# The first projection of a two-layer transformer kernel: chunk 0 normalized and transposed tile by tile, its weights loaded and split in another way

## Chip, cores, metric

One core of a Trainium2 chip. The metric is the device time of one execution in microseconds (us). Engines are named as in the profile: PE (TensorE matmuls), PEld (its weight loads), DVE (VectorE), ACT (ScalarE), POOL (GpSimd), SP (SyncE, which here only issues DMAs).

## What is computed

Two layers, each an attention block with one key/value head for 16 query heads, then a gated feed-forward block, all in f32, on x of 2048 rows by 448:

```python
x = A_x
for _ in range(2):
    x = x + A(layernorm(x), wq, wk, wv, wo)      # q: 16 heads of 28; k, v: one head of 28
    x = x + B(layernorm(x), w_gate, w_up, w_down) # (silu(g) * u) @ w_down, 1792 wide
```

The same weights serve both layers. The layer norm has no scale or shift: (x - mean) / sqrt(var + 1e-5).

## The kernel before

The 2048 rows are held in `xres` as 16 tiles of 128 rows, in four chunks of four tiles (512 rows). Every f32 matmul is done in three passes over operands split into a high half (rounded to fp32r) and a low half (the remainder): high x high, high x low, low x high. Names with h or hi hold high halves, names with l or lo low ones: `xh`/`xl` the normalized and transposed x of a chunk, `wh`/`wl` the projection's weights.

The order of the work is written out by hand: each engine runs its instructions in the order in which the code records them, and waits in place for what an instruction needs. DMAs are issued by SP and ACT; eight semaphores go round among them all, so that an issue also waits until the transfer that used its semaphore last has landed, and what stands behind it on that engine waits too.

The head of the program, layer 0's first projection, goes like this.

- Loads (L1104 on): the four tiles of chunk 0 of x, two by SP and two by ACT. Then `load_wqkv`: the projection's weights in two sets of 448 rows. Set z = 1 (tile `wr`, columns 224 to 447 of wq, and wk) is issued by ACT, set z = 0 (tile `wq` in the profile, `wq2` in the code; columns 0 to 223 of wq, and wv) by SP. `rows3` (L129) writes 448 rows as three blocks of 128 partitions and a fourth of 64 rows that is written twice, to partitions 0 to 63 and 64 to 127: three transfers a call.
- PE turns the identity 36 times (L1113) before there is any work.
- Normalization of chunk 0 (`norm_steps`, L211): statistics of the four tiles (DVE, L217 and L218), one rstd for all four columns (POOL: add eps at L222, power -0.5 at L223), the four tiles applied (DVE, L230), columns 384 to 447 of each written a second time (POOL, L232), so that block k = 3 holds its 64 rows twice.
- `parts[0]` splits set z = 1: ACT casts to `wh` (L190, once the wq columns, 128x896, once the wk columns, 128x128), POOL subtracts for `wl` (L192).
- `flip` transposes chunk 0 on PE (L248), four tiles for each k, into four PSUM banks; ACT casts each bank to `xh` (L254, L258), DVE subtracts for `xl` (L255) and for the lower half of k = 3 (L264).
- `project` runs the 16 products of the projection, one after the other: chunk c by column block m, order 3, 2, 0, 1 (m = 3 and 2 need set z = 1, m = 0 and 1 set z = 0). `product_T` (L304) is 11 matmuls of 128x512 into one bank. After a product, ACT copies it twice (L539, L540), SP stores it, and for m = 0 and 1 DVE turns 32 rows of it (`vt`, L547) and POOL copies them to `vsb`. Around the last product of a chunk the next chunk is transposed (`turned`): in layer 0 behind the whole of the fourth product with its copies, later ahead of the product. The statistics of chunks 1 to 3 are planned beside earlier products.
- `parts[1]` splits set z = 0: ACT casts, DVE subtracts. POOL fills constants (L1131 to L1138) meanwhile.

Later, attention runs as 128 cycles a layer of scores, exponentials and products with V, and the feed-forward block as 14 weight groups of 128 a layer. Their weights (`weights`) and the reloaded chunks (`fetch`, `back`) are read by `rows3` too. The kernel also holds a second, unshortened version of everything behind a branch that is taken only if a check on the exponentials fails; it is not run here.

Of the kernel before, what the change touches and what calls it, by code (L numbers as in the profile page):

```python
# [8 lines left out]
F32 = mybir.dt.float32  # L9
F32R = mybir.dt.float32r  # L10
AF = mybir.ActivationFunctionType
ALU = mybir.AluOpType
# [43 lines left out]
def forward(  # L56
# [72 lines left out]
    def rows3(dst, src, eng=nc.sync):  # L129
        eng.dma_start(dst[:, 0:3], src[0:384, :].rearrange("(k p) n -> p k n", p=P))  # L130
        for half in (slice(0, 64), slice(64, 128)):
            eng.dma_start(dst[half, 3], src[384:448, :])

# [34 lines left out]
    def load_wqkv(pool, first):  # L168
# [5 lines left out]
        def load(z):  # L174
            if first and not z:
                r = halves("wq2").bitcast(F32).rearrange("p a (b n) -> p (a b) n", n=256)
            else:
                r = wpool.tile([P, 4, 2, P], F32, name="wr").rearrange("p k b n -> p k (b n)")
            nc.gpsimd.memset(r[:, :, 252:256], 0.0)
            eng = nc.scalar if first and z else nc.sync  # L180
            rows3(r[:, :, 0:224], wq[:, 224 * z : 224 * z + 224], eng)
            rows3(r[:, :, 224:252], wk if z else wv, eng)
            return r

        def part(z, r):
            hi, lo = (w[:, :, 256 * z : 256 * z + 256].rearrange("p k (b n) -> p k b n", b=2) for w in (wh, wl))
            for cols, n0, n1 in ((r[:, :, 0:224], 0, 112), (r[:, :, 224:256], 112, 128)):
                raw = cols.rearrange("p k (b n) -> p k b n", b=2)
                if first:
                    nc.scalar.copy(hi[:, :, :, n0:n1], raw)  # L190
                    eng = nc.gpsimd if z else nc.vector
                    eng.tensor_tensor(lo[:, :, :, n0:n1], raw, hi[:, :, :, n0:n1], ALU.subtract)  # L192
                else:
                    split(hi[:, :, :, n0:n1], lo[:, :, :, n0:n1], raw)

        if first:
            r1, r0 = load(1), load(0)
            return [lambda: part(1, r1), lambda: part(0, r0)], (wh, wl)
        for z in (1, 0):
# [103 lines left out]

    def product_T(po, a_h, a_l, tiles):  # L304

        xh, xl = tiles[:2]
        seq = []
        for k in range(3):
            seq += [(a_h[k], xh[:, k, :]), (a_h[k], xl[:, k, :]), (a_l[k], xh[:, k, :])]
        seq += [(a_h[3], xh[:, 3, :]), (a_l[3], xh[:, 3, :])]  # L310
        for i, (a, b) in enumerate(seq):
            nc.tensor.matmul(po, a, b, start=(i == 0), stop=(i == len(seq) - 1))
# [30 lines left out]
    class Attention:  # L343
# [152 lines left out]
        def project(self):  # L496
# [6 lines left out]
            for o in turned if not late else ():  # L503
                self.turned(o)
            self.q(c, m)
            for o in turned if late else ():
                self.turned(o)
            for f in self.plan.get((self.seen, 1), []) + self.when.pop(self.seen, []):
# [6 lines left out]

        def q(self, c, m):
            cs = slice(512 * c, 512 * c + 512)
# [4 lines left out]
            wh, wl = self.w  # L522
            product_T(po, [wh[:, k, ms] for k in range(4)], [wl[:, k, ms] for k in range(4)], self.X[c])
            if not full and self.seen in (6, 10, 14):
# [587 lines left out]
    for n in range(IDLE):  # L1112
        nc.tensor.transpose(idle[:, 0:P], ident, ident)  # L1113
    parts, at.w = load_wqkv(xb.enter_context(tc.tile_pool(name="wqkv0", bufs=1)), True)
    nc.gpsimd.memset(halfn, -0.5)
    nc.scalar.activation(warm, halfn[:, 0:1], AF.Exp)
    nc.gpsimd.memset(bottom, 0.0)
    nc.gpsimd.memset(bottom[0:1, :], 1.0)
    fs, got = norm_steps(0)
    for f in fs[:5]:  # L1120
        f()
    for f in fs[5:]:
        f()
    parts[0]()
    at.norms[0] = got
# [3 lines left out]
    at.X = {c: xtile(xpool if c == 0 else xbp) for c in range(NC)}  # L1129
    at.turned(0)  # L1130
    nc.gpsimd.memset(vsb, 0.0)  # L1131
    nc.gpsimd.memset(vsb[:, :, DH : DH + 1], 1.0)
    nc.gpsimd.memset(qraw, 0.0)
    if mask is not None:
        nc.gpsimd.memset(mask, 0.0)
        nc.gpsimd.memset(mask[:, 0:16:5, :], 1.0)
        for base, sign in ((0, 1), (DH - 1, -1)):
# [3 lines left out]
            )  # L1141
    parts[1]()
    for c in range(1, NC):
# [40 lines left out]
```

## Time and profile before

| | |
|---|---|
| median of 3 runs | 1955.11 us (1954.94, 1955.11, 1956.85) |
| the profiled execution | 1957.93 us, span 1956.2 us |
| mean granted clock of PE | 0.998 |
| busy | PE 99%, PEld 68%, ACT 64%, DVE 50%, POOL 29% |
| PE waits for, up to 70 us, by what they wait for | 1.5 (identity), 1.1, 2.1, 0.7 (two waits), 0.3 us |

A timeline row gives the start from the beginning of the span, the duration (from the first start to the last end where "xN" rows are merged), engine, line, operation, written <- read tiles, and in brackets how long the engine sat idle before it and what ended that. ACTq and SPq are the DMA issues of those engines. A row of stages gives from:to, its length, then for PE, PEld, DVE, ACT and POOL the busy time with the number of instructions, then the granted clock, the DMA share and GB/s. A row of groups gives shapes and count, then busy us and mean ns of one, then the idle time ahead. A row of waits gives total, times, longest.

### The profile page before, as it was taken

Reading aid. Unit: us, or ns where it says so; the run is one execution under the profiler, and the core shown is the slowest. Engines: PE = TensorE matmul, PEld = TensorE weight load, DVE = VectorE, ACT = ScalarE, POOL = GpSimd, SP = SyncE. Lnnn points to the kernel's source line nnn. Section 1 sums busy time; section 2 is a strip of 40 time slices with the busy share of each in tenths; the row PEclk is TensorE's granted clock in tenths of the full one; section 3 lists DMA queues with packets and bytes.
Section 4 is the critical chain, followed back from the end, with each engine's and each line's share of the span. In section 5 each row is a group of like instructions: output and inputs, shape, how many; then the busy total and the mean of one; then the engine's idle time right before and its main releaser. Section 6 shows DMA issues by size and latency. Waiting matters only on the chain. (4 is left out here: it accounts for less than half of the span.)

```text
span 1956.2 us, 43857 instructions
## 1 busy us (share of the span) xinstructions
PE 1938.9 (99%) x18393; PEld 1335.2 (68%) x18393; DVE 976.9 (50%) x1643; ACT 1252.7 (64%) x1871; POOL 559.6 (29%) x596
## 2 busy tenths in 40 slices
PE   8999999999999999999999999999999999999998
PEld 7544544445469999999975445454454699988887
DVE  6665575665744222222655565657656532232323
ACT  4899898998953333333348998989989433333332
POOL 4213123122215333433332221122231252333420
PEclk9999999999999999999999999999999999999999
DMA  5111011021122011100251110110211221011102
GB/s 164 58 34 31 21 39 41 23 58 34 29 80 73 17 32 32 33 24 20 71 151 40 34 33 18 43 37 26 53 52 32 71 63 31 17 32 32 32 2 77
DMA packets 105475, 87.54 MB, mean 45 GB/s; under 512 B 25304, under 2 KB 85464, under 8 KB 105272
## 3 DMA queue, kind: packets, MB, share of 16 engines
q1 hardware_dynamic: 103576, 83.25, 15.1%
q8 instruction: 145, 2.38, 0.5%
q10 hardware_dynamic: 1696, 1.43, 0.2%
q14 instruction: 58, 0.48, 0.1%
HBM read 59.48 MB, written 23.33 MB: 42 GB/s over the span
## 5 line engine op out<-in xcount | busy, mean ns | idle before, releaser
L656 ACT ACTIVATE pt<-three 128x1536 f32<-128x1536 f32 x512 | 725.1, 1492 | 52.7 <-PE three L634 52.7
L689 PE MATMUL bank<-pt,vsb 128*32 128x512 f32 x3072 | 490.8, 598 | 0.0
L689 PE MATMUL bank<-pair,vsb 128*32 128x512 f32 x1024 | 487.3, 598 | 0.6 <-ACT pair L657 0.6
L634 PE MATMUL bank<-qstack,keys 32*128 32x512 f32 x1536 | 473.2, 424 | 0.0
L634 PE MATMUL three<-qstack,keys 32*128 32x512 f32 x4608 | 428.6, 408 | 0.5 <-ACT stage L540 0.3
L634 PEld LDWEIGHTS bank<-qstack,keys 32*128 32x128 f32 x1536 | 243.3, 183 | 250.3 <-issue 124.1
L655 DVE COPY pair<-bank 128x512 f32<-128x512 f32 x512 | 354.2, 692 | 95.1 <-PE bank L634 58.8
L332 PE MATMUL bank<-xh,wgh 64*128 64x512 f32 x1712 | 375.8, 389 | 0.0
L332 PE MATMUL bank<-xh,wgl 64*128 64x512 f32 x1391 | 324.1, 390 | 0.0
L1017 DVE TENSOR_TENSOR sg<-bank,sg 128x512 f32<-128x512 f32 x112 | 77.4, 691 | 491.0 <-ACT sg L1016 486.1
L332 PE MATMUL bank<-wdh,h 64*128 64x448 f32 x1760 | 311.6, 363 | 0.8 <-DVE h L1021 0.5
L657 ACT ACTIVATE pair<-pair 128x1024 f32<-128x1024 f32 x256 | 283.5, 1108 | 0.0
L332 PE MATMUL bank<-xl,wgh 64*128 64x512 f32 x1284 | 282.3, 389 | 0.0
L634 PEld LDWEIGHTS three<-qstack,keys 32*128 32x128 f32 x4608 | 261.1, 183 | 13.9 <-DVE xres L605 1.5
L689 PEld LDWEIGHTS bank<-pt,vsb 128*32 128x32 f32 x3072 | 101.7, 109 | 246.3 <-issue 153.2
L897 POOL TENSOR_TENSOR xres<-stage,xres 128x448 f32<-128x448 f32 x107 | 126.4, 1202 | 480.0 <-ACT stage L896 479.7
L698 DVE TENSOR_TENSOR o<-bank,o 128x512 f32<-128x512 f32 x224 | 154.9, 692 | 203.3 <-PE bank L689 203.3
L339 ACT COPY seen<-bank 128x1 f32<-128x1 f32 x654 | 74.9, 164 | 259.3 <-PE bank L332 258.5
L332 PEld LDWEIGHTS bank<-xh,wgh 64*128 64x128 f32 x1712 | 200.5, 184 | 12.2 <-issue 1.0
L332 PEld LDWEIGHTS bank<-wdh,h 64*128 64x128 f32 x1760 | 198.1, 184 | 11.6 <-issue 1.7
L1016 ACT ACTIVATE sg<-bank 128x512 f32<-128x512 f32 x112 | 67.3, 601 | 214.7 <-PE bank L332 211.5
L332 PE MATMUL bank<-wdl,h 64*128 64x448 f32 x880 | 184.1, 367 | 0.0
(147 smaller groups left out, 2144.7 us busy)
## 6 DMA issues: line engine op xcount, KB each, us to landing
o<-rd SPq DMA_DIRECT2D x32, 256.0 KB
qraw<-qd SPq DMA_DIRECT2D x128, 56.0 KB
xt<-tb SPq DMA_DIRECT2D x32, 224.0 KB
qd<-stage SPq DMA_DIRECT2D x28, 224.0 KB
wdr<-in_B_w_down_dram SPq DMA_DIRECT2D x28, 224.0 KB
xn<-xt SPq DMA_DIRECT2D x8, 768.0 KB
wr<-in_B_w_gate_dram SPq DMA_DIRECT2D x28, 192.0 KB
wr<-in_B_w_up_dram SPq DMA_DIRECT2D x28, 192.0 KB
```

The source lines that it names most:

```text
L332: nc.tensor.matmul(po, a, b, start=start, stop=stop, skip_group_check=True)
L339: nc.scalar.copy(seen[:, i : i + 1], po[:, 0:1])
L634: nc.tensor.matmul(three[:, j, :] if j < 3 else one, k[js, kp, ks], q[js, part, :], start=(z == 0), stop=(z == 2), tile_position=(32 * j, 0),)
L655: copies.append(nc.vector.tensor_copy(pt1, one))
L656: es.append(nc.scalar.activation(pt, threes[y], AF.Exp, scale=SCALE))
L657: es.append(nc.scalar.activation(pair, pair, AF.Exp, scale=SCALE))
L689: nc.tensor.matmul(to[32 * j : 32 * j + 32, :], vsb[:, n % NT, :], pts[n][j], start=(y == 0), stop=(y == 1), skip_group_check=True,)
L698: f = nc.vector.tensor_tensor(accs[i][:, 0, :], to, accs[i][:, 0, :], ALU.add)
L897: nc.gpsimd.tensor_tensor(r, s, r, ALU.add)
L1016: nc.scalar.activation(in_order(sg, True), natural(pg[0], True), AF.Silu)
L1017: nc.vector.tensor_tensor(in_order(sg, True), natural(pg[1], True), in_order(sg, True), ALU.mult)
```

## The change

- `rows3` writes the fourth block by one transfer that reads its 64 rows twice.
- Set z = 1's wq columns are issued by SP ahead of set z = 0; ACT issues only the wk columns.
- Chunk 0 is normalized tile by tile: each tile has its own add and power on a 128x1 column, and is applied as soon as the next tile's statistics are recorded. The second copy of columns 384 to 447 goes from POOL to ACT.
- The casts of set z = 1 stand on ACT between the second and third of these copies; its low halves are subtracted by POOL (wq columns) and DVE (wk columns). Set z = 0 is split on POOL alone, ahead of the constants.
- Chunk 0 is transposed tile by tile, each tile into all four banks.
- In the first product of layer 0 the four matmuls that read `wl` come last (`low_last`).
- Beside the fourth product the transposes and splits of chunk 1 are recorded behind its matmuls, ahead of its copies.

```diff
     def rows3(dst, src, eng=nc.sync):
         eng.dma_start(dst[:, 0:3], src[0:384, :].rearrange("(k p) n -> p k n", p=P))
-        for half in (slice(0, 64), slice(64, 128)):
-            eng.dma_start(dst[half, 3], src[384:448, :])
+        eng.dma_start(dst[:, 3], src[384:448, :][None].to_broadcast([2, 64, src.shape[1]]))
...
-            eng = nc.scalar if first and z else nc.sync
-            rows3(r[:, :, 0:224], wq[:, 224 * z : 224 * z + 224], eng)
-            rows3(r[:, :, 224:252], wk if z else wv, eng)
+            rows3(r[:, :, 0:224], wq[:, 224 * z : 224 * z + 224])
+            rows3(r[:, :, 224:252], wk if z else wv, nc.scalar if first and z else nc.sync)
             return r
 
-        def part(z, r):
+        def part(z, r, low=None):
             hi, lo = (w[:, :, 256 * z : 256 * z + 256].rearrange("p k (b n) -> p k b n", b=2) for w in (wh, wl))
             for cols, n0, n1 in ((r[:, :, 0:224], 0, 112), (r[:, :, 224:256], 112, 128)):
                 raw = cols.rearrange("p k (b n) -> p k b n", b=2)
-                if first:
-                    nc.scalar.copy(hi[:, :, :, n0:n1], raw)
-                    eng = nc.gpsimd if z else nc.vector
-                    eng.tensor_tensor(lo[:, :, :, n0:n1], raw, hi[:, :, :, n0:n1], ALU.subtract)
+                if first and z:
+                    if low is not True:
+                        nc.scalar.copy(hi[:, :, :, n0:n1], raw)
+                    if low is not False:
+                        eng = nc.vector if n0 else nc.gpsimd
+                        eng.tensor_tensor(lo[:, :, :, n0:n1], raw, hi[:, :, :, n0:n1], ALU.subtract)
                 else:
                     split(hi[:, :, :, n0:n1], lo[:, :, :, n0:n1], raw)
 
         if first:
             r1, r0 = load(1), load(0)
-            return [lambda: part(1, r1), lambda: part(0, r0)], (wh, wl)
+            return [lambda: part(1, r1, False), lambda: part(1, r1, True), lambda: part(0, r0)], (wh, wl)
...
-    def product_T(po, a_h, a_l, tiles):
+    def product_T(po, a_h, a_l, tiles, low_last=False):
...
+        if low_last:
+            seq = seq[0:2] + seq[3:5] + seq[6:8] + [seq[9], seq[2], seq[5], seq[8], seq[10]]
...
-            self.q(c, m)
-            for o in turned if late else ():
-                self.turned(o)
+            self.q(c, m, turned if late else ())
...
-            product_T(po, [wh[:, k, ms] for k in range(4)], [wl[:, k, ms] for k in range(4)], self.X[c])
+            product_T(
+                po, [wh[:, k, ms] for k in range(4)], [wl[:, k, ms] for k in range(4)], self.X[c],
+                low_last=self.layer == self.seen == 0,
+            )
+            for o in turned:
+                self.turned(o)
...
-    fs, got = norm_steps(0)
-    for f in fs[:5]:
-        f()
-    for f in fs[5:]:
-        f()
-    parts[0]()
+    fs, got = norm_steps(0, twice=False)
+    got["r"] = pers.tile([P, 4], F32, name="rstd", bufs=2)
+
+    def tile_rstd(t):
+
+        r = got["r"][:, t : t + 1]
+        nc.gpsimd.tensor_scalar(r, mv[:, t, 1:2], 1.0, EPS, ALU.mult, ALU.add)
+        nc.gpsimd.tensor_tensor(r, r, halfn[:, 0:1], ALU.pow)
+
+    def tile_apply(t):
+
+        fs[5 + t]()
+        nc.scalar.copy(got["x"][:, t, D:512], got["x"][:, t, 384:D])
+
+    for t in range(4):
+        fs[t]()
+        tile_rstd(t)
+        if t:
+            tile_apply(t - 1)
+        if t == 2:
+            wparts[0]()
+    tile_apply(3)
+    wparts[1]()
     at.norms[0] = got
...
-    at.turned(0)
+    pts = [bank(wide[-1])[1] for _ in range(4)]
+    for t in range(4):
+        for k in range(4):
+            nc.tensor.transpose(pts[k][:, P * t : P * t + P], got["x"][:, t, P * k : P * k + P], ident)
+    for k in range(4):
+        flipped(at.X[0], k, pts[k], nc.scalar.copy)
+    del at.norms[0]
+    wparts[2]()
...
-    parts[1]()
```

ACT's queue from its first weight issue to the first cast of chunk 0 (`wr` holds set z = 1, `xn` the normalized tiles, bank_87 the transposes of k = 0), before:

```order
L130 DMA wr<-in_A_wq_dram 128x3x224
L132 DMA wr<-in_A_wq_dram 64x224 x2
L130 DMA wr<-in_A_wk_dram 128x3x28
L132 DMA wr<-in_A_wk_dram 64x28 x2
L1116 ACT_TABLE_LOAD
L1116 ACTIVATE warm<-halfn 128x1
L190 CAST wh<-wr 128x4x2x112
L190 CAST wh<-wr 128x4x2x16
L254 CAST xh<-bank_87 128x512
```

and with the change:

```order
L130 DMA wr<-in_A_wk_dram 128x3x28
L131 DMA wr<-in_A_wk_dram 128x1x28
L1121 ACT_TABLE_LOAD
L1121 ACTIVATE warm<-halfn 128x1
L1136 COPY xn<-xn 128x64 x2
L189 CAST wh<-wr 128x4x2x112
L189 CAST wh<-wr 128x4x2x16
L1136 COPY xn<-xn 128x64 x2
L254 CAST xh<-bank_87 128x512
```

Two issues stand ahead of the table load instead of six, and four copies of 64 columns have come in around the two weight casts.

POOL's queue after the first fills (`rstd` is the normalization's factor, `mv` mean and variance, `wq_173` set z = 0), with the change; before, one add and one power on 128x4, the four copies to `xn`, and the two subtractions from `wr` stood ahead of the fills of `vsb`:

```order
L1130 TENSOR_SCALAR rstd<-mv 128x1
L1131 TENSOR_TENSOR rstd<-rstd,halfn 128x1
L192 TENSOR_TENSOR wl<-wr,wh 128x4x2x112
L134 TENSOR_SCALAR wh<-wq_173 128x4x2x112
L135 TENSOR_TENSOR wl<-wq_173,wh 128x4x2x112
L134 TENSOR_SCALAR wh<-wq_173 128x4x2x16
L135 TENSOR_TENSOR wl<-wq_173,wh 128x4x2x16
L1160 MEMSET vsb 128x512
```

The first two rows stand there four times in turn; the four rows on `wq_173` have come from ACT and DVE, ahead of the fills.

DVE's queue at chunk 1 (bank_85 and bank_86 hold the third and fourth product, banks 87, 88, 78, 79 the transposes of chunk 1), before:

```order
L547 STREAM_TRANSPOSE vt<-bank_85 32x512
L547 STREAM_TRANSPOSE vt<-bank_86 32x512
L255 TENSOR_TENSOR xl<-bank_87,xh 128x512
L255 TENSOR_TENSOR xl<-bank_88,xh 128x512
L255 TENSOR_TENSOR xl<-bank_78,xh 128x512
L264 TENSOR_TENSOR xh<-bank_79,xh 64x512
L409 TENSOR_TENSOR kdiag<-few,mask 112x512
```

and with the change:

```order
L552 STREAM_TRANSPOSE vt<-bank_85 32x512
L255 TENSOR_TENSOR xl<-bank_87,xh 128x512
L255 TENSOR_TENSOR xl<-bank_88,xh 128x512
L255 TENSOR_TENSOR xl<-bank_78,xh 128x512
L264 TENSOR_TENSOR xh<-bank_79,xh 64x512
L552 STREAM_TRANSPOSE vt<-bank_86 32x512
L411 TENSOR_TENSOR kdiag<-few,mask 112x512
```

The turn of the fourth product's rows has moved behind the four subtractions; the number of instructions is the same.

More of the change, by code (lines that the diff above doesn't have):

```diff
@@ L514, in turned, with q @@
                 flip(self.norms.pop(c), self.X[c])
-        def q(self, c, m):
+        def q(self, c, m, turned):
             cs = slice(512 * c, 512 * c + 512)
@@ L1113, in forward @@
         nc.tensor.transpose(idle[:, 0:P], ident, ident)
-    parts, at.w = load_wqkv(xb.enter_context(tc.tile_pool(name="wqkv0", bufs=1)), True)
+    wparts, at.w = load_wqkv(xb.enter_context(tc.tile_pool(name="wqkv0", bufs=1)), True)
     nc.gpsimd.memset(halfn, -0.5)
```

## The prediction

> **What bounds the kernel now.** I read the busy shares first, then the stages, then who TensorE (PE) waited for in the first 70 us, then the timeline.
>
> ```profile
> PE 1938.9 (99%) x18393; PEld 1335.2 (68%) x18393; DVE 976.9 (50%) x1643; ACT 1252.7 (64%) x1871; POOL 559.6 (29%) x596
> ```
> ```profile
> 10.00:20.00 10.00, 7.52 (x37) 5.70 (x37) 6.13 (x13) 6.27 (x12) 5.23 (x12) 1.00 0.83 290
> ...
> 70.00:100.00 30.00, 30.00 (x333) 13.28 (x332) 18.44 (x30) 30.00 (x25) 1.90 (x2) 1.00 0.05 14
> ```
> ```profile
> PE bank L312 <- ACT xh L254: 2.1, 1, 2.1
> ...
> PE bank L248 <- DVE xn L230: 1.1, 1, 1.1
> ```
> PE is busy 99% of the span, so only its idle time, or what makes it start later, can be saved by a change that leaves its matmuls alone. At 70 us attention begins with PE and ACT both full (30.00 of 30 us); what is ahead of it is a chain, and a chain that ends earlier moves everything behind it. The change touches that head. Its timeline (start, duration):
>
> ```profile
> 4.24 0.63 DVE L217 BATCH_NORM_STATS2 stats<-xres 128x6 f32<-128x448 f32 x1 [4.24 <-DMA xres<-in_A_x_dram]
> 4.90 0.18 DVE L218 BATCH_NORM_AGGREGATE mv<-stats 128x2 f32<-128x6 f32 x1
> 5.00 0.59 DVE L217 BATCH_NORM_STATS2 stats<-xres 128x6 f32<-128x448 f32 x1
> ...
> 7.08 0.18 DVE L218 BATCH_NORM_AGGREGATE mv<-stats 128x2 f32<-128x6 f32 x1
> 7.35 0.20 POOL L222 TENSOR_SCALAR rstd<-mv 128x4 f32<-128x4 f32 x1 [5.50 <-DVE mv L218]
> 7.64 1.03 POOL L223 TENSOR_TENSOR rstd<-rstd,halfn 128x4 f32<-128x4 f32 x1
> ...
> 8.71 1.78 DVE L230 TENSOR_SCALAR xn<-xres,mv,rstd 128x448 f32<-128x448 f32 x4 [1.44 <-POOL rstd L223]
> ...
> 9.27 0.14 PEld L248 LDWEIGHTS bank<-ident,xn 128*128 128x128 f32 x1 [1.38 <-DVE xn L230]
> ...
> 9.60 1.28 ACT L1116 ACT_TABLE_LOAD   x1 [9.60 <-DMA wr<-in_A_wk_dram]
> 9.70 0.14 PEld L248 LDWEIGHTS bank<-ident,xn 128*128 128x128 f32 x1 [0.29 <-DVE xn L230]
> ...
> 11.00 0.92 ACT L190 CAST wh<-wr 128x896 fp32r<-128x896 f32 x1
> ...
> 13.41 0.30 ACT L190 CAST wh<-wr 128x128 fp32r<-128x128 f32 x1 [1.49 <-DMA wr<-in_A_wk_dram]
> 13.62 1.56 ACT L254 CAST xh<-bank 128x512 fp32r<-128x512 f32 x3
> 14.23 1.89 DVE L255 TENSOR_TENSOR xl<-bank,xh 128x512 fp32r<-128x512 f32 x3 [3.74 <-ACT xh L254]
> ...
> 14.25 0.50 PE L312 MATMUL bank<-xh,wh 128*128 128x512 f32 x1 [2.07 <-ACT xh L254]
> ```
> The wait that ends last is not the normalization. DVE is done with xn at 10.49, but ACT stands behind its own DMA issues until 9.60 and then at a cast that waits for wk until 13.41; the casts of xh are queued behind it, and PE's first product starts at 14.25.
>
> **Part 1: when the first product starts.** ACT now issues four transfers without a wait and has its table loaded long before it is needed. What is late next is the last tile's normalization. The unknown is the power on 128x1. By the L222 row nothing there is under 0.20; the 128x4 power took 1.03, and these are the ends. Between them:
>
> ```profile
> L232 POOL COPY xn<-xn 128x64 f32<-128x64 f32 x16 | 5.8, 388 | 2.7 <-DVE xn L230 2.7
> ...
> L550 POOL COPY vsb<-vt 32x64 f32<-32x64 f32 x16 | 3.7, 234 | 5.7 <-DVE vt L547 5.1
> ...
> L192 POOL TENSOR_TENSOR wl<-wr,wh 128x896 fp32r<-128x896 f32 x1 | 2.1, 2072 | 1.2 <-ACT wh L190 1.2
> ...
> L192 POOL TENSOR_TENSOR wl<-wr,wh 128x128 fp32r<-128x128 f32 x1 | 0.5, 458 | 0.0
> ```
> The two L192 rows give (2072 - 458) / 768 = 2.1 ns a column and 0.19 us fixed. If the rest of the power's 1.03, 0.84, goes by element, one costs 0.21, and the instruction 0.40. I take 0.40, nearest to the rows of the same operation. The Trainium skill (GPSIMD Engine Reference, section 3.1) speaks against it: about 2.6 cycles an element, by which four elements cost some 9 ns and one would cost nearly the full 1.03, so the saving would be that of the upper end; that figure is for an add, and no run here shows a power on one column.
>
> The chain: tile 0's mean and variance stand at 5.08. POOL starts 0.09 later (7.26 to 7.35), 0.20, again 0.09, 0.40, and DVE 0.04 behind (8.67 to 8.71): tile 0 is applied at 5.90. An apply holds DVE for 0.42 (9.27 to 9.70), statistics and aggregate for 0.76 (4.24 to 5.00). So apply 1 starts at 7.08, the last statistics at 7.50, and they end at 7.50 + 0.84 = 8.34. Then 0.09 + 0.20 + 0.09 + 0.40 + 0.04: the last apply at 9.16. POOL's copies took 0.39 beside DVE's apply and 0.23 elsewhere, so I add 0.15: 9.31, against about 9.98 before. PE's transpose comes 0.56 behind (8.71 to 9.27), takes about 0.3 (estimate from the 16 in the 25.00 row below), ACT's xh 0.04 behind that, at 10.21, and the first product 0.63 later (13.62 to 14.25): **10.84 instead of 14.25, 3.41 us earlier**. ACT's four xn copies have no row; between nothing and the 0.30 of a cast twice as wide I take 0.25. They, and the weight casts of 0.92 and 0.30 between them, fit ahead of 10.21 if wr is there by 8.5.
>
> ```profile
> 7.01 1.64 SPq L132 DMA_DIRECT2D wq<-in_A_wv_dram  x2
> ...
> 8.20 1.37 ACTq L132 DMA_DIRECT2D wr<-in_A_wk_dram  x2
> ...
> 9.08 1.47 SPq L1102 DMA_DIRECT2D xres<-in_A_x_dram  x3
> ```
> Each of the first two rows starts when the 336 KB piece issued second behind x on its queue has landed: wq at 7.0, wr at 8.2. wr now has wq's place on SP; its last quarter (112 KB, one transfer instead of two) follows. I take 7.5. Chunk 1's x stays behind the same bytes on SP, so its issue is not past 9.08; 896 KB at the stage's 290 GB/s are 3.2 us, landed by about 14.
>
> **Part 2: inside product 1.** All four wl matmuls now come last, behind the one that waits for DVE's lower half of k 3.
>
> ```profile
> 16.15 0.69 DVE L264 TENSOR_TENSOR xh<-bank,xh 64x512 fp32r<-64x512 f32 x1
> ...
> 16.93 0.47 PE L312 MATMUL bank<-xh,wh 128*128 128x512 f32 x1
> ...
> 17.48 0.39 PE L312 MATMUL bank<-xh,wh 128*128 128x512 f32 x1
> ...
> 25.00 1.91 PE L248 MATMUL bank<-ident,xn 128*128 128x128 f32 x16
> ```
> Before, that matmul (16.93) came 2.68 after the first, as soon as DVE was done at 16.84, and one wl matmul was left: product 2 started at 17.48, 3.23 after the first. Now four are left. Three products took 25.00 - 17.48 = 7.52, 0.23 a matmul, so the three more cost **0.69**. The order buys nothing unless wl is late, and wl (2.07 on POOL from about 9.5) is there at 11.6, ahead of its first use at 13.8. Product 2 then starts at 14.76.
>
> Product 3 needs POOL's halves of wq. From 11.6, with every piece at L192's price (2.07 twice, 0.46 twice), they end at 16.7; product 3 starts at 14.76 + 2.5 = 17.3.
>
> ```profile
> 12.00 2.49 POOL L192 TENSOR_TENSOR wl<-wr,wh 128x896 fp32r<-128x896 f32 x2 [1.21 <-ACT wh L190]
> ...
> 15.92 0.78 POOL L1138 TENSOR_SCALAR_AFFINE_SELECT mask<-mask 128x64 f32<-128x64 f32 x2
> ```
> The fills behind it (14.49 to 16.70, 2.21 us), chunk 1's rstd (1.36) and apply (1.78) then end at 22.0; chunk 1's transposes are due at 25.00 - 2.72 = 22.3. Thin, but an upper bound. DVE's 1.1 us for wl of wq goes, ahead of work that had slack.
>
> **Part 3: chunk 1 ahead of the fourth product's copies.**
>
> ```profile
> 26.31 0.72 DVE L547 STREAM_TRANSPOSE vt<-bank 32x512 f32<-32x512 f32 x1 [1.24 <-ACT stage L540]
> ...
> 27.81 0.50 PE L312 MATMUL bank<-xl,wh 128*128 128x512 f32 x1 [0.50 <-DVE xl L255]
> ...
> 34.83 1.78 DVE L230 TENSOR_SCALAR xn<-xres,mv,rstd 128x448 f32<-128x448 f32 x4 [1.49 <-POOL rstd L223]
> ...
> 36.28 2.02 PE L248 MATMUL bank<-ident,xn 128*128 128x128 f32 x16
> ```
> xl of chunk 1 need no longer wait for vt and PE's 0.50 us stall goes, with the slow restart about 0.8 us. But vt is only moved behind xl. DVE then does the same work up to the end of chunk 2's apply at 36.61, and PE's transposes there (36.28, fourth one at 36.6) were already waiting for it: 16 took 2.02 instead of 1.91. DVE restarts when xh is cast, 26.25 by the durations, instead of 26.31. So **0.06 is kept**; the stall moves to chunk 2.
>
> The other rows3 calls lose a transfer in three in stretches where PE is full; I cost them at nothing, the cover being PE itself.
>
> **Sum.** 3.41 - 0.69 + 0.06 = 2.78 us. The profiled execution took 1957.93 with a span of 1956.2, so its span would be 1953.4; the median of the three runs, 1955.11, is 2.8 under that execution, and the same saving makes it **1952.3**. With the power at 0.20 the last apply is 0.40 earlier (two powers are on its path): 1951.9. At 1.03 POOL paces all four tiles at 1.36 each and the last apply is 1.44 later: 1953.8. The three runs lay 0.2 below to 1.7 above their median.
>
> **The rivals.** (a) Part 3's 0.75 us is kept: 1951.6. Against it speaks the 36.28 row. (b) The head's gain is swallowed further on: POOL misses chunk 1, or the chain from DVE to chunk 3 has no room: up to 1955.1. The 0.3 us margin above speaks for it, its upper bounds against. (c) Slower: wr lands late, since the one transfer for the last quarter does not bring it in sooner. ACT's casts (0.92 + 0.30) and two copies (0.5) stand ahead of xh, so xh is at the landing plus 1.7; it decides from 8.5, is even with before at 11.3, and as late as wk's last piece before (13.41) it gives xh at 15.1 and 1957.2. The 7.01 row speaks against.
>
> (d) PE's clock halves in the head, where it now has single transposes and half-filled products from 8 to 14 us.
>
> ```profile
> 1005.00:1010.00 5.00, 2.85 (x6) 2.03 (x7) 3.32 (x5) 2.86 (x5) 0.93 (x4) 0.67 0.64 175
> 1010.00:1020.00 10.00, 10.00 (x43) 8.15 (x43) 1.58 (x3) 4.16 (x8) 6.61 (x10) 0.82 0.45 136
> ```
> ```profile
> PE bank L312 <- ACT xh L292: 3.1, 1, 3.1
> ```
> One wait of 3.1 us at 1004 us was followed by a granted clock of 0.67 and 0.82: (0.33 x 5) + (0.18 x 10) = 3.45 us of clock lost. In the head that gives 1955.8. The waits I expect there are under 1.2 us, and a 2.1 us wait before (14.25) left the clock at 1.00. (e) The same dip may depend on where the wait falls against whatever window decides it; the shift of 2.8 us could make it go: 1948.9. The Trainium skill (TensorE: Matmul & The Clock Gate, part 1) has the clock halved after an idle window of some 3.4 us that runs freely; a 3.1 us wait would then never fill one, yet the trace shows the dip, so a part of a window suffices here, and the phase can matter.
>
> **How the numbers follow.** Forecast 0.55, (a) 0.07, (b) 0.10, (c) 0.05, (d) 0.08, (e) 0.15. The range 1951.0 to 1956.0 takes in the forecast's ends with the runs' spread, (a), (b) and (d); (c) and (e), 0.20, are left out. About 0.2%, 3.9 us, is what a measurement of this kernel can tell from no change: under 1951.2 are (e), and 0.07 from (a) and the forecast's lower end, 0.22; over 1959.0 the far end of (c) and (d), 0.05; within it 0.73.
>
> **What would show it.** First product near 10.8, product 2 near 14.8 with PE waiting ahead of the seventh matmul, no wait for wl; the 128x1 power near 0.40; the 27.8 stall gone and chunk 2's transposes stretched by 0.8; the start of attention 2.8 us earlier. It is wrong if ACT waits for wr, if the power stays near 1 us, if POOL makes product 3 wait, or if the granted clock at 1007 us changes.

## The result and the profile after

The changed kernel took **1961.71 us** (median of 7 runs, 1960.12 to 1964.0), the kernel before 1955.38 beside it (7 runs, 1954.7 to 1956.85): a ratio of 1.003, 95% interval 1.0021 to 1.004. It is slower by some 6 us. 1952.3 was predicted, and the range ended at 1956.0. The profiled execution of after took 1963.31 with a span of 1961.6.

First the head, read as in the prediction (start, duration, engine, line; lines past 130 have moved by up to 5):

```profile
5.74 0.57 POOL L1131 TENSOR_TENSOR rstd<-rstd,halfn 128x1 f32<-128x1 f32 x1
...
8.95 4.61 SPq L1107 DMA_DIRECT2D xres<-in_A_x_dram  x3
...
9.66 1.14 ACT L189 CAST wh<-wr 128x896 fp32r<-128x896 f32 x2 [1.37 <-DMA wr<-in_A_wq_dram]
9.96 0.51 DVE L230 TENSOR_SCALAR xn<-xres,mv,rstd 128x448 f32<-128x448 f32 x1 [0.72 <-POOL rstd L1131]
10.68 2.10 POOL L192 TENSOR_TENSOR wl<-wr,wh 128x896 fp32r<-128x896 f32 x1 [0.75 <-ACT wh L189]
10.83 2.09 DVE L192 TENSOR_TENSOR wl<-wr,wh 128x128 fp32r<-128x128 f32 x1 [0.36 <-ACT wh L189]
...
11.47 1.56 ACT L254 CAST xh<-bank 128x512 fp32r<-128x512 f32 x3 [0.38 <-PE bank L1155]
12.11 0.49 PE L314 MATMUL bank<-xh,wh 128*128 128x512 f32 x1 [0.35 <-ACT xh L254]
...
13.57 0.79 PE L314 MATMUL bank<-xl,wh 128*128 128x512 f32 x1 [0.97 <-DVE xl L255]
...
25.01 1.91 PE L248 MATMUL bank<-ident,xn 128*128 128x128 f32 x16
```

ACT waits for wr until 9.66, where by the prediction 8.5 was the latest that did no harm; that ACT waits for wr was also its first sign of being wrong. The first product starts at 12.11: 2.1 us earlier than in the profile of before, and 1.3 later than predicted. And the 2.1 us are gone by 25.01, where chunk 1's transposes stood at 25.00 before. They go inside the first product. PE waits 0.97 for xl, which stands on DVE behind the lower half of wk (2.09). The later order of the wl matmuls takes its share. And two rows of the windows (stretches of time) show the clock: PE was busy for 1.26 of 3.42 us, and in the next stretch of the same length it ran at half clock, about 1.7 us of clock lost (half of 3.41).

```profile
10.04:13.46 3.42, 1.26 (x6) 0.71 (x6) 3.06 (x4) 3.04 (x8) 2.14 (x2) 1.00 0.45 98
13.46:16.87 3.41, 3.30 (x8) 2.58 (x9) 2.58 (x6) 0.07 (x1) 3.27 (x3) 0.50 0.98 333
```

So between these two traces the head costs nothing and brings nothing. (In two further profiles of before, shown under l1 to l4, chunk 1 stands at 23.99 and 23.49; against them after's head is 1.0 to 1.5 us late.) The rest is lost where the prediction did not look. Who PE waits for, whole span of after (us in total, times, longest); of before the first was 0.4 in two waits, and the other two were not in the list:

```profile
PE bank L334 <- DMA xd<-xh: 3.8, 2, 2.4
...
PE three L618 <- POOL onl L135: 1.4, 2, 0.7
...
PE three L618 <- POOL onh L134: 1.0, 2, 0.5
```

The same rows in the three traces place it (e1, below, is after with the old pair of transfers):

| what starts | before | after | e1 |
|---|---|---|---|
| chunk 1's transposes | 25.00 | 25.01 | 25.40 |
| ninth addition into xres at L605, layer 0 | 464.25 | 465.90 | 464.91 |
| first matmul on xd, layer 0 | 586.03 | 588.93 | 586.75 |
| SP's fetch of the last chunk for layer 1 | 1000.82 | 1002.77 | 1001.85 |
| ninth addition into xres at L605, layer 1 | 1433.22 | 1435.37 | 1432.69 |
| first matmul on xd, layer 1 | 1555.01 | 1559.57 | 1554.53 |
| last matmul | 1950.80 | 1955.89 | 1950.27 |

After is 1.65 us behind at 464. It loses about as much again at 1433 (PE's waits for onh and onl are two each; that the distance is only 2.15 there is because before ran for 6.83 us at half clock near 1007, and after for 3.41), and 2.4 more up to 1555. A like loss at layer 0's xd (2.90 behind at 589) does not last: some 20 us later the distance is 1.8 again. In layer 1 it stays, and there after runs for another 3.41 us at half clock, from 1559.69. How it comes about at 464, from the timelines, before and then after:

```profile
455.99 1.05 POOL L135 TENSOR_SCALAR wgh<-wr 128x1024 fp32r<-128x1024 f32 x1 [0.91 <-ACT pt L656]
...
461.25 0.63 POOL L135 TENSOR_SCALAR onh<-o 128x512 fp32r<-128x512 f32 x1
```
```profile
458.02 1.06 POOL L134 TENSOR_SCALAR wgh<-wr 128x1024 fp32r<-128x1024 f32 x1 [3.90 <-DMA o<-moved]
...
463.30 0.62 POOL L134 TENSOR_SCALAR onh<-o 128x512 fp32r<-128x512 f32 x1
463.97 0.19 PEld L618 LDWEIGHTS three<-woh,onh 128*128 128x128 f32 x1 [0.85 <-POOL onh L134]
...
465.33 0.19 PEld L618 LDWEIGHTS three<-woh,onl 128*128 128x128 f32 x1 [1.06 <-POOL onl L135]
```

POOL starts the split of the feed-forward's weights 2.03 us later. The bracket names o<-moved, but the split reads only wr: the traces' semaphore records have wr's last piece complete at 457.88, in before at 455.77, and the split starts 0.14 and 0.22 behind. POOL works in order, and behind that split stands onh, which is 2.05 later, and for onh PE waits. PE was full, and it was no cover: the late transfer was ahead of an engine that PE needs next.

At the two transitions the fetch of xn is late. The DMA view between 555 and 575 us, in slices of half a microsecond (the digit is the busy share of the 16 DMA engines in tenths), before, e1 and then after:

```profile
DMA  9799980000000001000010012222200000000001
```
```profile
DMA  6959999300000001100001000122221000000000
```
```profile
DMA  0068799911111111122100000001001122220000
GB/s 16 21 78 176 193 377 406 348 29 41 53 49 49 53 53 49 49 57 82 21 0 0 0 0 0 0 3 14 0 0 20 61 106 102 102 98 33 0 0 0
```
```profile
565.28 0.62 ACT L296 CAST xh<-xn 128x512 fp32r<-128x512 f32 x1 [3.66 <-DMA xn<-xt]
```

That is the whole case in one line. Behind the nines, the transfer of the first three blocks at about 400 GB/s, stands a row of ones: some 5 us at about 50 GB/s. That is an eighth of 400, so two of sixteen DMA engines. The fourth block's 256 KB take that long (256 KB / 50 GB/s = 5.2 us), and ACT waits 3.66 us for them. With the pair of transfers, in before and in e1, no such row follows the nines. The head has the same stretch from 8 to 12 us (0 to 20 us, in the same slices):

```profile
DMA  0003959999999982171111119499999799999999
GB/s 0 0 0 22 68 161 376 398 394 390 375 327 194 311 279 73 47 111 45 43 47 47 48 45 109 86 320 389 401 401 265 204 290 383 412 330 369 405 401 398
```

### The profile page after: what moved, and what is told of

Read it like the earlier page. It is cut to its first block, busy times and chain, and to the rows that moved or that the text cites. A ratio compares the mean times of both kernels' runs of the same rounds, so it can differ in the third digit from the quotient of the medians.

```text
span 1961.6 us, 43728 instructions
## 1 busy us (share of the span) xinstructions
PE 1940.6 (99%) x18393; PEld 1329.4 (68%) x18393; DVE 977.3 (50%) x1642; ACT 1259.2 (64%) x1873; POOL 564.5 (29%) x601
## 5 line engine op out<-in xcount | busy, mean ns | idle before, releaser
L334 PE MATMUL bank<-xh,wgh 64*128 64x512 f32 x1712 | 443.7, 389 | 0.0
L334 PE MATMUL bank<-xh,wgl 64*128 64x512 f32 x1391 | 366.9, 390 | 0.0
L334 PE MATMUL bank<-xl,wgh 64*128 64x512 f32 x1284 | 333.1, 390 | 0.0
L334 PE MATMUL bank<-wdh,h 64*128 64x448 f32 x1760 | 329.2, 364 | 0.1
L334 PEld LDWEIGHTS bank<-xh,wgh 64*128 64x128 f32 x1712 | 264.7, 185 | 14.5 <-issue 0.7
L334 PEld LDWEIGHTS bank<-wdh,h 64*128 64x128 f32 x1760 | 246.1, 184 | 11.2 <-issue 1.7
L341 ACT COPY seen<-bank 128x1 f32<-128x1 f32 x654 | 80.5, 163 | 247.4 <-PE bank L334 244.8
L334 PEld LDWEIGHTS bank<-xh,wgl 64*128 64x128 f32 x1391 | 217.7, 184 | 13.0
L334 PE MATMUL bank<-wdl,h 64*128 64x448 f32 x880 | 218.5, 367 | 0.0
```

Of the source, the lines that this page charges most:

```text
L334: nc.tensor.matmul(po, a, b, start=start, stop=stop, skip_group_check=True)
L341: nc.scalar.copy(seen[:, i : i + 1], po[:, 0:1])
```

## The experiments

**T1**, the theory: the one broadcast transfer is slow. **R1**, its rival: POOL and DVE beside each other and the clock cost the head, and the later waits come of the new phase. Four runs tell them apart, all timed against before on one chip (before: 1956.51, 1955.14 to 1958.91).

**e1**, after with the pair of transfers back:
```diff
-        eng.dma_start(dst[:, 3], src[384:448, :][None].to_broadcast([2, 64, src.shape[1]]))
+        for half in (slice(0, 64), slice(64, 128)):
+            eng.dma_start(dst[half, 3], src[384:448, :])
```


> The changed kernel, with the fourth block again in two transfers of 64 rows, everywhere. Theory T1 (the one transfer for the fourth block is slow: in the trace of after its semaphore is raised by few late increments and wr's last piece lands at 9.58 where 7.5 was taken; in the feed-forward's weights and in the fetch of xn it is late by 2 to 4 us and POOL and PE wait behind it): the waits at 463, 585, 1432 and 1555 us go (1.7 + 0.1 + 1.9 + 2.7 = 6.4 us) and the head's gain comes out, between nothing (if the clock still dips in the head) and 2.8 us: 1952.5 to 1955.5, first product near 11.2. Rival R1 (POOL and DVE beside each other, with the clock's dip, cost the head; the later waits come from the new phase): the lower half of wl still takes 2 us on DVE, the waits at 463 and 1432 us stay, 1959 to 1962.

Measured: 1957.91, ratio 1.0007 (0.9998 to 1.0017). The four late waits are gone (xd back at 0.5, no onh or onl):
```profile
PE bank L335 <- DMA xd<-xh: 0.5, 2, 0.3
```
T1 is right on those. But the head's gain did not come out, the median is 1.4 us over that of before; see e4.

**e2**, before with nothing but the one transfer (the same two lines the other way).

> The kernel before, with nothing but the fourth block in one broadcast transfer. T1: the waits at 463, 585, 1432 and 1555 us appear, 4 to 6.5 us of them, and the head is later too (ACT's cast of wk and DVE's of wq wait for their last pieces): 1959 to 1963. Rival R1: nothing to see, within 1 us of the kernel before (1954.5 to 1956.5).

Measured: 1969.02, ratio 1.0063 (1.005 to 1.0077), 12 us slower, about twice the most that T1 asked for. The waits on xd (4.4), onl (1.4) and onh (0.8) are there. The rest is in the head: ACT's casts of wr wait 5.51 and 1.47 us for their pieces, PE's first product waits 3.5 us for xh, and the clock is down for three stretches of 3.41 us, from 11.78 to 22.02. This row lies inside (the granted clock is the third number from the end):
```profile
15.00:20.00 5.00, 3.28 (x7) 2.38 (x8) 3.24 (x5) 3.28 (x7) 3.92 (x9) 0.50 0.79 277
```

**e3** and **e3b**, after with the one transfer in the head alone, and everywhere but in the head:
```diff
-    def rows3(dst, src, eng=nc.sync):
+    def rows3(dst, src, eng=nc.sync, head=False):
...
+        if head:    # e3b: if not head
```


> The changed kernel with the one broadcast transfer for the four pieces of layer 0's wq, wk and wv in the head alone, two transfers of 64 rows elsewhere. T1: the head is that of after (no gain at 25 us), the four later waits are gone: 1954.5 to 1956.5, 1 to 3 us above e1. R1: as e1.

> The mirror of the one before: two transfers of 64 rows in the head, the one broadcast transfer everywhere else. T1: the head is that of e1, the four later waits stay (6.4 us): 1958 to 1961, and e3 plus e3b together lie as far from e1 as the changed kernel does, give or take the clock. R1: as e1.

Measured: e3 1957.74, 1.0007 (0.9998 to 1.0016); e3b 1965.01, 1.0039 (1.0025 to 1.0052). So **most of the slower time is made outside the head**: 7.1 us between e3b and e1, and nothing between e3 and e1. (e3b lies above after's 1.003, but the intervals overlap.) In e3b's list, where onl and onh stand as well, with 1.4 and 0.8:
```profile
PE bank L338 <- DMA xd<-xh: 3.8, 2, 2.9
```
T1's part on the head fails: the late wr costs e3 nothing against e1, because e1 loses its head in another way. This is how, in e1's timeline:
```profile
9.97 2.07 POOL L193 TENSOR_TENSOR wl<-wr,wh 128x896 fp32r<-128x896 f32 x1
10.04 2.25 DVE L231 TENSOR_SCALAR xn<-xres,mv,rstd 128x448 f32<-128x448 f32 x1 [0.71 <-POOL rstd L1132]
...
12.34 0.66 PE L1156 MATMUL bank<-ident,xn 128*128 128x128 f32 x4 [2.31 <-DVE xn L231]
...
13.34 0.49 PE L315 MATMUL bank<-xh,wh 128*128 128x512 f32 x1 [0.35 <-ACT xh L255]
```
wr is there early, so POOL starts its big subtraction at 9.97, just ahead of DVE's last apply, and the apply takes 2.25 us where the three before it took 0.48 to 0.51. It ends 0.25 behind POOL's end at 12.04. In after it was DVE's 128x128 subtraction that took 2.09 (one of that shape took 0.28 in before), ending 0.14 behind POOL. R1 was right on this pair.

Four more runs (e4 to e7) take the head apart, on one chip with before (1955.21, 1954.15 to 1959.07).

**e4**, e1 with POOL kept out of DVE's way:
```diff
-        nc.scalar.copy(got["x"][:, t, D:512], got["x"][:, t, 384:D])
+        (nc.gpsimd.tensor_copy if t == 3 else nc.scalar.copy)(got["x"][:, t, D:512], got["x"][:, t, 384:D])
...
-                        eng = nc.vector if n0 else nc.gpsimd
-                        eng.tensor_tensor(lo[:, :, :, n0:n1], raw, hi[:, :, :, n0:n1], ALU.subtract)
+                        nc.gpsimd.tensor_tensor(lo[:, :, :, n0:n1], raw, hi[:, :, :, n0:n1], ALU.subtract)
```


> e1 with two moves to POOL: the copy of the fourth tile's last 64 columns (from ACT), so that POOL's lower half of wl can only start behind DVE's last apply, and the lower half of wk (from DVE). Theory T2 (in e1 the head's gain is lost because DVE's last apply takes 2.25 us where the others take 0.5: it and POOL's 128x896 subtraction want the same way to SBUF and it waits until POOL is done): the last apply takes 0.5 again, first product at 11.6 instead of 13.34, product 4 ends near 23.5 instead of 25.2, the time 1.2 to 3.4 under e1, by whether the clock's dip in the head goes too: 1954.5 to 1956.7. Rival R2 (the apply was slow for another reason, or POOL's longer list makes product 3 wait): the first product stays past 13 or product 3 waits 1 us or more, the time within 0.7 of e1.

Measured: 1954.69, ratio 0.9995 (0.9986 to 1.0004). T2's first product, 11.6, is right to a tenth:
```profile
9.93 0.51 DVE L230 TENSOR_SCALAR xn<-xres,mv,rstd 128x448 f32<-128x448 f32 x1 [0.72 <-POOL rstd L1131]
...
10.70 2.52 POOL L192 TENSOR_TENSOR wl<-wr,wh 128x896 fp32r<-128x896 f32 x2
...
11.50 0.50 PE L314 MATMUL bank<-xh,wh 128*128 128x512 f32 x1 [0.35 <-ACT xh L254]
...
22.94 1.25 PE L248 MATMUL bank<-ident,xn 128*128 128x128 f32 x10
```
The apply takes 0.51 beside no one, the first product comes 1.84 us earlier, the clock does not dip in the head, and chunk 1's transposes are at 22.94.

**e5**, e1 with 14 transposes of the identity where PE waits, and **e6**, e4 with 2, 4 and 4 of them behind the second, third and fourth tile:
```diff
+        for n in range((0, 0, 14, 0)[t]):    # e6: (0, 2, 4, 4)
+            nc.tensor.transpose(idle[:, 0:P], ident, ident)
```


> e1 with 14 transposes of the identity into a spare bank behind the third tile's transposes, where PE waits 2.3 us. Theory T3 (the clock halves for 3.41 us behind a stretch of 3.41 us in which PE was busy under about half, and e1's head has one at 10.4 to 13.8, busy 0.32): the granted clock is 1.00 from 10 to 20 us, 1.7 us gained less 0.2 for the last fillers: 1.5 under e1, 1956.4, if the dip near 1007 us does not come instead. Rival R3 (the dip comes from the power drawn, or from the half-filled products): it stays, and the time is that of e1 or 0.2 over it.

> e4 with 2, 4 and 4 transposes of the identity behind the second, third and fourth tile's, against the clock's dip. T2 and T3: first product near 11.7, clock at 1.00 up to 1000 us, product 4 ends near 22.8, chunk 1 is then the next thing PE waits for (its x lands near 16, its transposes can start near 22.3): 1953.5 to 1955.5. If chunk 1 or DVE's chain up to chunk 3 swallows it: as e4.

Measured: e5 1956.67, 1.0005 (0.9996 to 1.0014); e6 1954.78, 0.9995 (0.9986 to 1.0004). e5 refutes T3 as it was put: PE was busy for 2.04 of 3.41 us, more than half, and the clock halved all the same.
```profile
10.78:14.19 3.41, 2.04 (x13) 1.25 (x11) 3.31 (x4) 1.84 (x5) 3.33 (x3) 1.00 0.94 299
14.19:17.61 3.42, 3.42 (x9) 2.45 (x9) 3.29 (x8) 0.46 (x1) 3.15 (x9) 0.50 1.04 402
```
In before a stretch with 1.98 was followed by full clock (its granted clock is 1.00 from 10 to 20 us):
```profile
10.01:13.42 3.41, 1.98 (x15) 1.54 (x14) 0.48 (x2) 1.91 (x4) 2.20 (x4) 1.00 0.92 296
```
So busy time alone, as the profile has it, does not decide. e6's head is the best measured: first product at 11.23, chunk 1 at 22.67; its time is e4's.

**e7** and **e10** put the first product's matmuls back in the old order, in e4 and in e6 (e10 with before at 1955.9 on its chip):
```diff
-                low_last=self.layer == self.seen == 0,
+                low_last=False,
```


> e4 with the first product's matmuls in the old order (each lower half of the weights right behind the upper). By the prediction's second step the order costs 0.69 and buys nothing unless wl is late: 0.7 under e4. Rival: wl, on POOL from 10.8 to 12.9, is needed at 12.3 by the old order; PE waits 0.6 there and the time is that of e4.

> e6 with the first product's matmuls in the old order, without a clock dip in the way. The prediction's second step: 0.69 less 0.4 (the wait for POOL's wl that e7's profile shows) = 0.3 under e6; product 2 starts 3.2 to 3.6 behind product 1 instead of 3.93 (15.16 - 11.23). Rival: the order is worth its place, PE waits longer for wl than 0.7: the time of e6 or more.

Measured: e7 1956.23, 1.0005 (0.9996 to 1.0014), with the clock's dip back in its profile, so it says nothing on 0.7 us; e10 1954.91, 0.9994 (0.9985 to 1.0003). e10's rows, of product 1's start, its third matmul and product 2's start:
```profile
11.56 0.49 PE L314 MATMUL bank<-xh,wh 128*128 128x512 f32 x1
...
13.34 0.50 PE L314 MATMUL bank<-xh,wl 128*128 128x512 f32 x1 [0.56 <-POOL wl L192]
...
15.54 0.40 PE L314 MATMUL bank<-xh,wh 128*128 128x512 f32 x1
```
Product 2 comes 3.98 behind product 1, and in e6 3.93 (11.23 to 15.16). The times do not tell the two orders apart; by these rows the rival is right: with POOL's wl late the old order waits for about as much as the new order costs. The 0.69 is real (three more matmuls of 0.23 at the end) and buys its price back.

**e8**, e6 with chunk 1's transposes behind the fourth product's copies again (on e10's chip, as e9 and e11):
```diff
-            self.q(c, m, turned if late else ())
+            self.q(c, m, ())
+            for o in turned if late else ():
+                self.turned(o)
...
-            for o in turned:
-                self.turned(o)
```


> e6 with the third part of the change undone: chunk 1's transposes come behind the fourth product's copies again. The prediction's third step: the stall at chunk 1 is back (0.5 to 0.8 us at 24 to 25 us) and the one at chunk 2 goes, 0.06 lost in all: the time of e6, 1954.8, within what can be told. Rival (a) of the prediction: the part is worth 0.75: 0.75 over e6.

Measured: 1954.88, 0.9997 (0.9988 to 1.0006). The stall moves as forecast; e8 and then e6:
```profile
25.68 0.50 PE L314 MATMUL bank<-xl,wh 128*128 128x512 f32 x1 [0.50 <-DVE xl L255]
...
34.09 2.09 PE L248 MATMUL bank<-ident,xn 128*128 128x128 f32 x16
```
```profile
33.09 2.83 PE L248 MATMUL bank<-ident,xn 128*128 128x128 f32 x16
```
e8 stalls 0.50 at chunk 1, and chunk 2's transposes take 2.09; e6 has no stall there, and they take 2.83. In the two traces e8 is 0.21 behind e6 at chunk 1's transposes and 0.26 at chunk 3's, so the part brings 0.05. In the medians it is worth nothing that can be measured.

**e11**, e6 with one rstd for the chunk's four tiles (of the transposes that fill PE's waits, eight move ahead of all work and four stay behind the last tile):
```diff
-        tile_rstd(t)
...
+    nc.gpsimd.tensor_scalar(got["r"], mv[:, 0:4, 1], 1.0, EPS, ALU.mult, ALU.add)
+    nc.gpsimd.tensor_tensor(got["r"], got["r"], halfn, ALU.pow)
```


> e6 with chunk 0's rstd computed once for all four tiles, as before, and applied then (the filling transposes moved ahead of it). Theory T4 (the head's gain comes from ACT's queue, that no longer issues wk and wr's transfers and loads its table early, not from the tile by tile normalization): the last apply starts at 8.71 + 3 x 0.445 = 10.04 where e6 has 9.66, the first product 0.3 to 0.5 later than e6's 11.23, the time 0.3 to 0.5 over e6: 1955.2. Rival R4 (tile by tile is what makes the gain): the first product past 12.5, 1.3 us or more over e6.

Measured: 1955.64, 0.9998 (0.9989 to 1.0007).
```profile
8.98 1.78 DVE L230 TENSOR_SCALAR xn<-xres,mv,rstd 128x448 f32<-128x448 f32 x4 [1.44 <-POOL rstd L1135]
...
11.86 0.49 PE L314 MATMUL bank<-xh,wh 128*128 128x512 f32 x1
```
The first product is 0.63 later than in e6, a little more than T4 gave: the chain runs 0.27 behind that of before (8.98 against 8.71). R4's 12.5 is refuted: the tile by tile normalization brings the first product 0.3 to 0.6 us (11.23, 11.32 and 11.52 in three profiles of e6). That ACT's earlier casts are worth the rest of the head's gain is argued from the queue; it was not tried alone.

**l1 to l4**: if the head is 2.3 us earlier in e6, why is its median only 0.4 us under that of before? Two more profiles of before and two of e6.

> The kernel before, unchanged, for a second profile. In the fourteen profiles so far the last chunk's way through DRAM (from SP's first issue at layer 1's last fetch to ACT's cast, near 1001 us) took 4.01 to 5.65 us without any order by the change, and the first profile of before has the longest. Theory T6 (of e6's gain of 2.3 us at the head only 0.4 to 1 is seen in the medians because PE waits for that way in either kernel, and the chances of the way and the clock decide the rest): the way is shorter this time, 4.0 to 5.0, the execution 1954 to 1956, SP's issue again at 1000.5 to 1001. Rival R6 (the first profile of before was late by 990 us already): SP's issue comes at 999.5 or earlier.

> The same a third time. T6: issue at 1000.5 to 1001 again, the way anything from 4.0 to 5.65. R6: issue at 999.5 or earlier.

> e6 for a second profile. T6: head as in the first (product 4 ends at 22.7), issue at 998.7 to 999.1, the way 4.0 to 5.65, the execution 1953 to 1956 by it and by the clock near 1005 us. R6: the gain of the head is not there in every execution: product 4 ends past 23.5, or the issue comes past 999.5.

> The same a third time, with the same numbers by each theory.

Measured: before 1956.10 and 1955.13, e6 1954.24 and 1955.08, one execution each. **The first profile of before was late already in its head, and that undercuts the prediction's first number.** SP's issue comes at 999.84 and 999.38 in before, where it was 1000.82: the second is what R6 asked for, the first lies between the two forecasts. In e6 it comes at 998.88 and 999.29, with the head as in the first profile, which is T6's side. The second and then the third profile of before:
```profile
10.75 1.12 ACT L190 CAST wh<-wr 128x896 fp32r<-128x896 f32 x2
...
12.41 0.51 PE L312 MATMUL bank<-xh,wh 128*128 128x512 f32 x1
...
23.99 1.91 PE L248 MATMUL bank<-ident,xn 128*128 128x128 f32 x16
```
```profile
11.93 0.48 PE L312 MATMUL bank<-xh,wh 128*128 128x512 f32 x1
...
23.49 1.91 PE L248 MATMUL bank<-ident,xn 128*128 128x128 f32 x16
```
Neither has the wait for wk until 13.41. wk's last piece was late in the one execution that the prediction was worked out from; why, no run shows. The first product of before starts at 11.9 to 12.4 in the other two and chunk 1 at 23.5 to 24.0, so the repaired head (22.67, 22.74 and 22.95 in e6's three profiles) gains 0.5 to 1.3 us, not 2.3. Against the same two, the heads of after (25.01) and of e1 (25.40) are 1.0 to 1.9 us late, which goes with e1's median of 1.4 us over before.

T6's other half is seen too. The way of the last chunk through DRAM near 1001 us took 5.65, 5.17 and 4.94 us in the three profiles of before and 4.22, 4.50 and 5.25 in those of e6, and the clock halved behind the wait in five of the six.

**e9** and **e12**, e6 with 8 transposes of the identity against that dip; e9's stood four products too late and told nothing of it (1954.81, 0.9996, 0.9987 to 1.0005).
```diff
+            for n in range(8 if self.layer and self.seen == 8 else 0):    # e9: 12
+                nc.tensor.transpose(po[:, 0:P], ident, ident)
```


> e6 with 8 transposes of the identity ahead of the thirteenth product of layer 1, where PE waits 1.6 to 3.1 us near 1004 us. T3: the clock can no longer halve there, whatever the phase; the runs of e6 that have the dip (1.7 us each, some of it hidden) come down to those that have not: median 0.3 to 1.2 under e6, 1953.6 to 1954.5, and less spread. R3: the time of e6.

> e9 with its 8 transposes where they were meant to be: ahead of the ninth product of layer 1, whose wait near 1003 us they precede (in e9 they came four products behind it, at 1021 us). T3: the window around the wait gets 1.4 us more of PE's work, the granted clock stays 1.00 near 1005 us and the median falls 0.3 to 1.2 under e6's, relative to before 0.9990 or less. R3: the clock halves there all the same, or the runs that had no dip lose what the others gain: 0.9993 to 0.9998 of before, as e6.

Measured: e12 1954.43 (1953.93 to 1955.30), beside it before 1956.29; ratio 0.9992 (0.9983 to 1.0001). The window near 1003 us is filled and the clock stays whole:
```profile
1002.29 1.03 PE L524 MATMUL bank<-ident 128*128 128x128 f32 x8
1003.85 0.50 PE L314 MATMUL bank<-xh,wh 128*128 128x512 f32 x1 [0.53 <-ACT xh L292]
...
1005.00:1010.00 5.00, 5.00 (x22) 3.86 (x22) 1.72 (x3) 1.70 (x4) 2.77 (x5) 1.00 0.54 176
```
Its runs lie within 1.4 us of each other, those of e6 within 3.1. T3's 0.9990 was not reached, and e6's 0.9995 lies inside the interval; the run points T3's way and does not settle it. e12 is the best version found, though its interval still takes in no change from before; against after (1.003) it is about 7 us faster by the two ratios, taken on two chips.

## Why the prediction was wrong

**The step that failed** is the transfer, in two places. In Part 1: "its last quarter (112 KB, one transfer instead of two) follows. I take 7.5." ACT had it at 9.66. In Part 3: "The other rows3 calls lose a transfer in three in stretches where PE is full; I cost them at nothing, the cover being PE itself." e1 and e3b put 7 us on it. Both places took one transfer to be no worse than two by its bytes, and neither asked how the bytes are spread. The rows of ones (two of sixteen engines, 50 GB/s instead of 400) are what a broadcast of 2 as the outermost dimension does here; in two transfers of 64 rows each spread over all sixteen. The traces' semaphore records agree: wr's last quarter in after counts up by two late steps, 9.43 and 9.58, and each of the pair's two transfers in e1 by sixteen, complete at 7.61 and 7.77. So for the pair the 7.5 was nearly right. The Trainium skill has the rule, which the prediction did not use: in DMA: Bandwidth & Descriptors, section "Why a DMA increments its semaphore by 16 and not by 1", a DMA runs on the largest number of engines up to 16 that divides the outermost dimension of both access patterns, and section "Rules for kernel authors" names the leading broadcast of c copies as confined to c engines. The trace agrees: 2 of 16. The same table of the Trainium skill advises one transfer instead of two halves, which alone would have spoken for the change.

This step is what made the kernel slower. That the 2.78 us did not come with the pair back either (e1, 1957.91) has other causes, under the base and the sizes below.

**The cover** was argued from PE's share, and a full PE is no cover for a transfer that POOL or ACT takes ahead of PE: POOL's queue carried the 2 us from the weights to onh, and ACT waited 3.66 us for xn ahead of xh.

**The rivals.** (c) was what happened in the head: it took xh at the landing plus 1.7, 9.66 + 1.7 = 11.36, and xh came at 11.47. It had 0.05 and no price outside the head. (d) happened as well, with 3.41 us at half clock, about 1.7 us of clock lost where (d) had put 3.45. (b)'s place was wrong: e4 and e6 carry their head's gain unchanged past chunk 3 into attention. (e) is not borne out as a gain of the change: the dip near 1007 differs between executions of one kernel (6.83, 3.41 and 3.41 us in three profiles of before; none, 3.41 and 3.41 in three of e6).

**The base.** 3.41 us were to be won against a first product at 14.25. In two further profiles of before it starts at 12.41 and 11.93, so 1.8 to 2.3 us of the gain were one execution's late transfer (1.0 to 1.5 at chunk 1, since PE then waits 0.7 for wl inside the product). The row with the wait of 1.49 us for wk was true, and it was not typical. The sum then took a saving worked out from that execution, 1957.93, off the median of 1955.11, whose executions need not have had it to lose.

**The sizes.** The 128x1 power took 0.55 to 0.61, not 0.40; the last apply of e6 is at 9.66 (9.31 predicted), the first product at 11.23 (10.84). DVE's lower half of wk, which the prediction did not price, took 2.09 beside POOL in after; in e1, DVE's last apply took 2.25 in the same way. POOL began wl at 10.68 in after (about 9.5 predicted), so it was ready at 12.8 and not at 11.6. The order of the first product costs its 0.69 and gets it back (e10). The third part's 0.06 is borne out by the rows (0.05), with the stall moved to chunk 2 as forecast (e8).

## What to carry to other kernels

Count a transfer by the DMA engines it runs on, not by its bytes or its number: put a dimension that sixteen divides outermost (here the 64 rows, not the 2 copies), and look for a stretch of ones in the DMA row. Work out a gain from more than one profile of the kernel before when a wait for a DMA is its largest term, since that wait may belong to one execution. And a stretch with a full engine hides a late transfer only if that engine's next inputs do not stand in order behind it.

## What the runs showed of the hardware

- DVE beside POOL: DVE's 128x448 tensor_scalar took 2.25 us and its 128x128 subtraction 2.09 when POOL's 128x896 subtraction had started up to 0.15 us earlier, 0.51 and 0.28 without. DVE's xl subtractions, whose raw operand is in PSUM, kept their 0.63 beside the same POOL instruction. The Trainium skill (SBUF — State Buffer, section "SBUF: two separate sides") has DVE and GpSimd share one pair of ports as a lock held for a whole instruction; the rows agree, down to the end 0.14 to 0.25 behind POOL's.
- The power of 128x1 on POOL took 0.55 to 0.61 where that of 128x4 took 1.03: if it goes by element, (1.03 - 0.57) / 3 = 0.15 us each.
- The clock halved for stretches of 3.41 us (and of twice and three times that). By the traces' records of the granted clock, all such stretches of one trace start on one grid with a step of 3.413 us. With the 19 traces cut at this grid, every stretch at full clock in which PE was busy for under 1.5 us was followed by half clock (1.26 of 3.42 in after), and none in which it was busy for over 2.1. Between them both occur: half behind 2.04 (e5), full behind 1.98 (before) and 1.51 (e1, at 1003.64). So 1.4 us without work in 3.41 can be enough, and what decides in between is open. Out of half clock it took more: behind a half-clock stretch the clock stayed at half up to 2.96 us busy (before, at 1006.69) and once at 3.11 (e3b), and was full again from 3.18 on and once at 3.06 (e7).
- The three issues of x on SP took 4.61 us in after, 1.69 in e1, whose only difference is the pair of transfers, and 1.47 in before. So issues take longer behind the slow transfer; what holds them is not shown.
